# A new order of issue for the first block of an attention and gated MLP kernel

## The chip, the cores and the metric

The kernel runs on one core of one Trainium2 chip. The core has five engines, each with its own queue of instructions that it works off in order: TensorE (PE, matrix products; PEld is its weight load), VectorE (DVE), ScalarE (ACT), GpSimd (POOL) and SyncE (SP), which here issues the loads and most stores. SBUF is the working memory with 128 partitions; PSUM holds the results of TensorE in eight banks of 512 float32 columns. The metric is device time in microseconds (us). Before the change, three runs took 926.85, 927.66 and 929.27 us; the median is 927.66.

## The reference

Attention over eight batches of eight heads, 576 positions of 64 numbers, and then a gated MLP over all 4608 rows of 512 numbers:

```python
scores = q @ k.T / 8                      # per batch and head
heads 0-3: keep 0 <= rel < 32             # local: the last 32 positions
heads 4-7: keep rel >= 0, same pos % 32   # strided
attn = softmax(scores) @ v                # (8, 8, 576, 64)
x    = attn laid out as (4608, 512)
out  = (sigmoid(x @ w_gate) * (x @ w_val)) @ w_out    # 512 -> 1536 -> 512
```

All inputs and outputs are float32.

## The kernel before

**Attention** is done for pairs of heads. A batch has four pairs, numbered 0 to 3: 0 and 2 are local, 1 and 3 strided. A pair's scores are small products of its queries and keys (up to 64 columns each), laid into two banks over a mask that another product has put there. DVE takes the row maximum and subtracts it, ACT takes the exponential, DVE sums the rows and takes the reciprocal, DVE or POOL multiplies; TensorE turns the result (in batch 0) or DVE does (later), ACT copies it from PSUM, and TensorE weighs the values with it in 44 or 72 tiny products. The outcome is one of the four 128-row chunks of the MLP's input for that batch.

**The MLP** takes 512 rows of a batch at a time against 12 units of 128 hidden columns. Every product of float32 numbers is made of three faster ones: both factors are split into a high and a low part, and high x high, high x low and low x high are summed. Three such matmuls of 512 columns for one 128-row chunk of the input are called a *quarter product* here; four chunks make a gate or value product of one unit. Batches 3 to 7 use a scheme with fewer products, which the change leaves alone.

**Weights** are loaded raw (512 KB per matrix and unit, three matrices per unit) and split during the first and second batch: ACT makes an upper and a lower word (line 257 and line 261), DVE shifts (265), DVE or POOL puts them together (269), ACT rounds the high part (273), and DVE or POOL subtracts to get the low part (276).

**The order of the work** is one list, `ORDER` (line 78), of some 2360 short names. The program goes through it once and calls one function per name (`STEPS`); every instruction of the step is appended to the queue of its engine. So the list fixes the order on each engine, and semaphores make an engine wait where its next instruction needs something that another has not finished. Loads of all kinds share SP's queue. The names for the first block, `b.p` being batch and pair, `f.i` unit and matrix (0 gate, 1 value, 2 output):

- `K` constants; `fQ`, `fQa`, `fQb` load of queries and keys (whole, first part, second part); `fV` load of values; `wr` load of raw weights (all on SP)
- `C` identity matrix on POOL; `fZ` clears paddings on POOL
- `fK`, `fKa` mask and `fS`, `fSa` scores (PE); `fA`, `fAa` maximum, `fU`, `fUa` subtraction (DVE); `fE`, `fEa` exponential (ACT); `fN` sum and reciprocal (DVE); `fW` multiplication on DVE, `fWp` on POOL; `fT` transposes (PE); `fP` their copy (ACT); `fX` weighing (PE); `fH` high part (ACT) and `fL` low part (DVE) of the MLP's input; `fR` rows kept for the end (ACT); `fB`, `fM` transposes and masks on DVE in batch 1
- `wa`, `wb` upper and lower words (ACT); `ws` shift (DVE); `wd` on DVE or `wdp` on POOL, put together; `wu` high part (ACT); `wl` on DVE or `wlp` on POOL, low part
- `fg f.i.c` quarter product of batch 0, where c is the pair whose chunk it takes; `fg f.i` all four
- `s` sigmoid, `m` gating, `x`, `y` split of the hidden rows, `o` output product; `e` eviction of an output, `d` its store
- `J n` fill: matmuls of n columns of ones whose result nobody reads. They go to a tile in bank g, the same bank that `fg 0.0` uses, and need only a tile of ones that POOL sets at `J0`.

`BANKS` (line 64) says which pair of PSUM banks (a, o0 or o1) a step of the first block uses; a step not named there uses a. A step that writes a bank waits until the readers of its former contents are done. The step's instructions: a fill of 512 columns is a float32 matmul at line 730; scores are line 371, masks 358, transposes 467 and 471, weighing 513, gate and value products 592, output products 623.

Of the kernel before, what the change touches and what calls it, by code (L numbers as in the profile page):

```python
# [90 lines left out]
wd6.1 wr8.1 x0.4 y0.4 wu6.1 ws5.2 wa7.0 wlp6.1 o0.3 wd5.2 s0.5 wb7.0 wb7.1 ws7.0 wu5.2 wa7.1 wl5.2 fg5.1 ws7.1 wb6.2 wd7.1 wd7.0 wu7.1 fA1.1 wu7.0
wlp7.1 fg6.0 wa6.2 m0.5 ws6.2 x0.5 wa8.1 y0.5 wb8.1 wd6.2 fg6.1 wr9.0 wl7.0 s0.6 wu6.2 ws8.1 wb8.0 wl6.2 fU1.1 wa7.2 wa8.0 fg7.0 m0.6 wr8.2 ws8.0 x0.6
ws7.2 wb7.2 y0.6 wd8.0 fg7.1 wd7.2 s0.7 wu8.0 wd8.1 wu7.2 wl8.0 wl7.2 o0.4 m0.7 fE1.1 wa8.2 fN1.1 wb8.2 wu8.1 ws8.2 wr9.1 fWp1.1 wa9.0 fg8.0 wb9.0
ws9.0 x0.7 wr9.2 wdp8.2 fB1.1.2 fB1.1.3 o0.5 wlp8.1 s0.8 wu8.2 fB1.1.1 wlp8.2 wb9.1 wa9.1 fB1.1.0 wr10.0 fg8.1 wa9.2 wb9.2 ws9.1 wd9.1 wr10.1 wd9.0
wu9.1 y0.7 wu9.0 wlp9.1 o0.6 wl9.0 m0.8 wa10.0 fS1.2 ws10.0 wb10.1 ws9.2 wdp9.2 wb10.0 fg9.0 fM1.2 fQ1.3 wa10.1 wr10.2 x0.8 wdp10.0 wr11.0 fA1.2 wu9.2
fU1.2 wlp9.2 wu10.0 o0.7 y0.8 fE1.2 wlp10.0 fn1.2 fg9.1 fN1.2 s0.9 fW1.2 wa10.2 wb10.2 ws10.1 wd10.1 wr11.1 wa11.0 fX1.1 ws10.2 wb11.0 ws11.0 m0.9
wu10.1 wdp11.0 wr11.2 o0.8 fH1.1 fV1.2 fR1.1 fL1.1 x0.9 wlp10.1 fB1.2.0 wdp10.2 wu11.0 fB1.2.3 fg10.0 wlp11.0 fB1.2.1 wu10.2 fB1.2.2 wb11.1 fS1.3
s0.10 y0.9 fZ1.3 wlp10.2 wa11.1 fg10.1 fM1.3 LQ0 fA1.3 fU1.3 fX1.2 ws11.1 fE1.3 m0.10 wdp11.1 fN1.3 fg11.0 fH1.2 fV1.3 fR1.2 fW1.3 wu11.1 x0.10
wlp11.1 fB1.3.3 o0.9 fB1.3.2 s0.11 wb11.2 fL1.2 wa11.2 fB1.3.0 fg11.1 fB1.3.1 y0.10 ws11.2 fX1.3 m0.11 wd11.2 x0.11 o0.10 fH1.3 LV0 y0.11 wu11.2 fL1.3
pa0.0.0 fR1.3 wl11.2 pa0.0.1 g1.0 pl0 pb0.0.0 v1.0 s1.0 pb0.0.1 oh0.11.0 m1.0 x1.0 S0.0 e0.0 y1.0 d0.0 oh0.11.1 LQ1 M0.0 M0.1 D0 A0 g1.1 U0 e0.1 E0  # L100
d0.1 e0.2 N0 v1.1 d0.2 W0 s1.1 B0.3 g1.2 m1.1 e0.3 x1.1 B0.1 ph0.0.0.1 d0.3 y1.1 v1.2 B0.0 s1.2 B0.2 ph0.0.1.0 Z1 o1.0 m1.2 pw0.0.0 x1.2 pw0.0.1
pd0.0.0 y1.2 pd0.0.1 X0.0 S1.0 LV1 H0 R0 L0 o1.1 LQ2 M1.0 pa0.1.0 M1.1 D1 A1 pa0.1.1 U1 g1.3 E1 pb0.1.0 N1 W1 v1.3 s1.3 pb0.1.1 ph0.1.0.1 B1.2 B1.0
# [965 lines left out]
```

## Time and profile before

| | |
|---|---|
| median of three runs | 927.66 us (926.85 to 929.27) |
| the profiled execution | 929.75 us, its span from first to last instruction 927.6 us |
| TensorE busy | 919.8 us, 99% of the span |
| VectorE, ScalarE, GpSimd busy | 599.9, 426.8, 179.9 us |
| fills (line 730) | 20 records, the last starting at 17.9 us |
| first quarter product | 22.82 us |
| first output product `o0.0` | 49.93 us on the chain that ended last |

A row of the profile names the line, engine, operation, what is written and from what, the count, and times. A row of the timeline starts with its start and its length in us, and ends, where the engine was idle before, with that idle time and who released it. A row of stretches gives the length, then busy time and number of instructions of PE, PEld, DVE, ACT and POOL, then the granted TensorE clock as a share of full speed (PEclk), the share of the DMA engines in use, and GB/s. TensorE counts as busy while a matmul is in it, at either clock. A float32 matmul shows as two records.

### The profile page before, as it was taken

The page shows a single profiled execution, that of the slowest core. Times are in us where ns is not written, and L with a number is a line of the kernel's source. Part 1 is how long each engine was busy: PE and PEld are TensorE (multiplying, and loading weights), DVE is VectorE, ACT ScalarE, POOL GpSimd, SP SyncE. Part 2 cuts the span into 40 slices and gives each one's busy share as a digit, 9 for nine tenths or more (in the row PEclk, how much of TensorE's full clock was granted, in tenths as well). Part 3 has the DMA queues.
Part 4 walks back from the last instruction along what each step waited for, and adds up shares of the span by engine and source line. Part 5 has one row for each costly group of instructions (what it writes and reads, how often), then busy time and mean ns, then how long its engine had stood idle before and what let it go on. Part 6 is the DMA issues. An engine that isn't in the chain of part 4 may idle for free.

```text
span 927.6 us, 18516 instructions
## 1 busy us (share of the span) xinstructions
PE 919.8 (99%) x7606; PEld 754.9 (81%) x7606; DVE 599.9 (65%) x959; ACT 426.8 (46%) x776; POOL 179.9 (19%) x243
## 2 busy tenths in 40 slices
...
PEclk9899999999999999999999999999999999999999
...
GB/s 345 333 220 85 197 152 153 159 192 159 199 240 247 115 187 191 208 189 181 193 157 181 149 109 195 198 181 148 138 156 125 23 174 178 145 150 146 59 45 46
DMA packets 90195, 154.19 MB, mean 166 GB/s; under 512 B 5888, under 2 KB 40192, under 8 KB 90112
## 3 DMA queue, kind: packets, MB, share of 16 engines
...
## 4 chain that ended last, share of the span: by engine, by line
PE 98%; ACT 1%; DVE 1%; issue 0%; POOL 0%; DVEq 0%; ACTq 0%; POOLq 0%
PE o L623 22%; PE p L887 21%; PE d L887 16%; PE g L592 10%; PE v L592 10%; PE o_a L623 5%; PE o_g L623 3%; PE o_v L623 3%; PE x_a L513 2%; PE x L513 1%; PE s_g L371 1%; PE s_v L371 1%; PE gv L592 1%; PE s L371 1%; PE unread L730 0%; ACT sb L435 0%
## 5 line engine op out<-in xcount | busy, mean ns | idle before, releaser
L887 PE MATMUL p<-xs,ring 128*128 128x512 f32 x864 | 204.6, 389 | 0.0
L887 PEld LDWEIGHTS p<-xs,ring 128*128 128x128 f32 x864 | 162.2, 188 | 33.7
L623 PE MATMUL o<-w,hh 128*128 128x512 f32 x576 | 180.6, 395 | 0.0
L887 PE MATMUL d<-xs,ring 128*128 128x512 f32 x648 | 155.6, 389 | 0.0
L887 PEld LDWEIGHTS d<-xs,ring 128*128 128x128 f32 x648 | 121.6, 188 | 25.2
L623 PEld LDWEIGHTS o<-w,hh 128*128 128x128 f32 x576 | 106.1, 188 | 22.7
L480 DVE STREAM_TRANSPOSE pt<-sb 32x320 f32<-32x320 f32 (+1 forms) x224 | 120.1, 536 | 4.5
L623 PE MATMUL o<-w,hl 128*128 128x512 f32 x288 | 112.0, 389 | 0.0
L921 DVE TENSOR_TENSOR e<-e,d 128x512 f32<-128x512 f32 x54 | 37.1, 687 | 110.6 <-PE d L887 62.5
L592 PE MATMUL g<-xh,w 128*128 128x512 f32 x256 | 85.9, 393 | 0.0
L916 ACT COPY e<-p 128x512 f32<-128x512 f32 x54 | 31.7, 587 | 116.8 <-PE p L887 116.8
L592 PE MATMUL v<-xh,w 128*128 128x512 f32 x256 | 85.2, 390 | 0.0
L623 PEld LDWEIGHTS o<-w,hl 128*128 128x128 f32 x288 | 54.1, 188 | 11.5
L592 PEld LDWEIGHTS g<-xh,w 128*128 128x128 f32 x256 | 48.5, 189 | 10.3
L592 PEld LDWEIGHTS v<-xh,w 128*128 128x128 f32 x256 | 48.0, 188 | 10.0
L815 POOL TENSOR_TENSOR sum<-sum 128x128 f32<-128x128 f32 x96 | 51.5, 540 | 6.3
L592 PE MATMUL g<-xl,w 128*128 128x512 f32 x128 | 50.3, 393 | 0.3 <-DVE xl L553 0.3
L616 DVE TENSOR_TENSOR hl<-hid,hh 128x512 fp32r<-128x512 f32 x36 | 28.0, 780 | 34.5 <-ACT hh L612 34.3
L592 PE MATMUL v<-xl,w 128*128 128x512 f32 x128 | 49.8, 389 | 0.0
L810 POOL TENSOR_TENSOR sum<-w 128x256 f32<-128x256 f32 x44 | 35.5, 827 | 72.7 <-DMA sets<-sum 49.4
L929 ACT ACTIVATE e<-e 128x512 f32<-128x512 f32 x54 | 34.2, 633 | 29.9 <-DVE e L921 29.9
L612 ACT CAST hh<-hid 128x512 fp32r<-128x512 f32 x36 | 22.4, 622 | 49.9 <-PE o_a L623 41.1
...
## 6 DMA issues: line engine op xcount, KB each, us to landing
ring<-sets SPq DMA_DIRECT2D x126, 512.0 KB, 4.1
raw<-in_w_all SPq DMA_DIRECT2D x36, 512.0 KB, 5.8
vv<-in_v_l SPq DMA_DIRECT2D x15, 640.0 KB, 4.6
qk<-in_qk_l SPq DMA_DIRECT2D x14, 608.0 KB, 5.2
...
```

Source lines behind the costliest of these rows:

```text
L371: nc.tensor.matmul(sc[j % len(sc)][g * m : (g + 1) * m, j // len(sc) * BANK + (s - lo) * kk : j // len(sc) * BANK + (s - lo + 1) * kk], q[ ...
L480: nc.vector.transpose(dst[to : to + LB, :, col : col + LB], src[part * LB : (part + 1) * LB, :, h * LB : (h + 1) * LB])
L513: nc.tensor.matmul(at_bank(r, (u * per + g) * m, (u * per + g + 1) * m)[j * D : (j + 1) * D], v[part][rows, slot * P + j * D : slot * P + ...
L592: nc.tensor.matmul(o, w, x, start=first and n == 0, stop=last and n == len(todo) - 1)
L616: by.tensor_tensor(hl, whole_h.pop((k, f)), hh.bitcast(F32), op=ALU.subtract)
L623: nc.tensor.matmul(acc[k][i], h[:, i * P : (i + 1) * P], w, start=f == 0 and n == 0, stop=f == NF - 1 and n == 2,)
L810: nc.gpsimd.tensor_tensor(u[:, at : at + 2], part(wh[f][i], c), part(wl[f][i], c), op=ALU.add)
L815: nc.gpsimd.tensor_tensor(u[:, to], u[:, x], u[:, y], op=op)
L887: nc.tensor.matmul(to, w[:, (wi * 2 + c) * P : (wi * 2 + c + 1) * P], x[xi][:, c], start=p in (1, 2, 5) and c == j == 0, stop=c == 1 and j ...
L916: nc.scalar.copy(x, two[m, 0])
L921: nc.vector.tensor_tensor(x, x, two[m, 1], op=ALU.add)
L929: nc.scalar.activation(x, x, AF.Sigmoid)
```

## The change

The list is replaced from its first step up to the last steps of the weights and sums of unit pairs (batch 2's last MLP units); from there on it is the same but for single steps. No function changes, and no step's work; the names differ in these ways:

- Fills: J576, J352, J1024, J1088, J256 and J256 are replaced by J384, J160, J1184, J160, J128, J480 and J160.
- Loads: the constants come first, pair 0.2 is loaded ahead of 0.1, and weights 0.1, 0.0, 1.0 and 1.1 come ahead of 2.0 and 2.1; before it was 2.0, 1.0, 0.0, then the values, then 0.1 and 1.1.
- Order of the pairs on the engines: 0.0, 0.2, 0.1, 0.3, with the transposes and the weighing of 0.0 ahead of the scores of 0.1 and 0.3.
- The multiplication of pair 0.2 goes to POOL, those of 0.0, 0.1 and 0.3 to DVE (before: 0.0 and 0.1 on POOL); that of pair 1.3 goes to POOL.
- Weights: `wd` 20 to 17, `wdp` 16 to 19, `wl` 15 to 19, `wlp` 21 to 17 instructions.
- `BANKS`: the banks that the first block's steps use are given anew.
- Further on, six evictions `e` and their stores `d` stand one or a few places earlier (e2.2, e3.2, e4.2, e5.2, e6.3, e7.3 with their neighbours), and two rounding steps of sums (`ph`) use another buffer.

```diff
-    "S0.0": "o0", "T0.0": "o1", "X0.0": "o1", "S0.1": "o1", "T0.1": "o0", "X0.1": "o0", "S0.2": "o1", "X0.2": "o1", "T0.3": "o0", "X0.3": "o0",
+    "Sa0.0": "o0", "S0.0": "o1", "T0.0": "o0", "S0.1": "o1", "T0.1": "o1", "T0.2": "o0", "X0.2": "o0", "S0.3": "o0", "T0.3": "o0", "X0.3": "o0",
...
-fQb0.0 fZ0.0 fZ0.1 J0 K fZ0.3 fZ0.2 fQa0.0 fQa0.1 fQb0.1 wr2.0 fQ0.2 wr1.0 fQ0.3 C J576 fK0.1 wr0.0 fV0.1 fKa0.0 fV0.0 fK0.0 fV0.2 J352 fSa0.0 fV0.3 wr0.1 fS0.0
-fAa0.0 wr1.1 fSa0.1 fA0.0 fQ1.0 wr0.2 fUa0.0 wr2.1 fS0.1 fU0.0 fEa0.0 wr1.2 fK0.3 fE0.0 fA0.1 wb2.0 wa2.0 fU0.1 wr4.1 fN0.0 fE0.1 J1024 fK0.2 fS0.2 fN0.1
-fWp0.0 wa1.0 wb1.0 fA0.2 fWp0.1 wr3.1 fU0.2 J1088 fS0.3 ws1.0 fE0.2 ws2.0 wdp1.0 fT0.1 fN0.2 wa0.0 wb0.0 ws0.0 J256 fT0.0 fA0.3 wr2.2 fP0.1 wdp0.0 wu1.0 fW0.2
-J256 fX0.1 fP0.0 wlp1.0 wu0.0 fU0.3 fX0.0 fH0.1 wd2.0 fR0.1 wlp0.0 fE0.3 fL0.1 fT0.2 fH0.0 fV1.0 fR0.0 wu2.0 fL0.0 fN0.3 wlp2.0 fg0.0.0 fP0.2 fX0.2 fW0.3
-wb0.1 wa0.1 fg1.0.0 fH0.2 ws0.1 wr3.0 wb1.1 fT0.3 fL0.2 wa1.1 wd0.1 fR0.2 wr3.2 ws1.1 fg0.0.1 fP0.3 wd1.1 fS1.0 wu0.1 wu1.1 wl0.1 wb0.2 wlp1.1 fg1.0.1
-fM1.0 fQ1.1 wa0.2 fg0.1.0 fA1.0 wr4.0 fg0.0.2 wa2.1 fU1.0 fg0.1.1 wb2.1 ws2.1 fX0.3 fE1.0 wr4.2 ws0.2 wdp2.1 wb1.2 fn1.0 fg1.1.0 fH0.3 fN1.0 wu2.1
-fg0.1.2 fL0.3 fWp1.0 wa1.2 fg1.1.1 fR0.3 ws1.2 wr5.0 fg1.0.2 wlp2.1 fB1.0.1 fg0.0.3 fg0.1.3 fB1.0.0 s0.0 wdp0.2 fg1.0.3 wb2.2 m0.0 wa2.2 fg1.1.2
-wdp1.2 fB1.0.2 x0.0 wr5.1 fg2.0.0 s0.1 fg2.1.0 y0.0 wu0.2 fg2.0.1 wu1.2 fB1.0.3 wa3.0 fg1.1.3 wb3.0 ws2.2 fZ1.1 fg2.1.1 m0.1 wdp2.2 wr5.2 fg2.0.2
-wl0.2 x0.1 fX1.0 wb3.2 y0.1 wa3.1 ws3.0 fg2.1.2 fH1.0 fV1.1 wd3.0 wb3.1 fg2.0.3 ws3.1 fR1.0 fL1.0 wr6.0 fg2.1.3 wdp3.1 s0.2 fS1.1 wu3.0 m0.2 wlp3.0
-wu3.1 wl1.2 x0.2 o0.0 fQ1.2 wa4.0 wa3.2 wl3.1 wb4.0 wr6.1 y0.2 wu2.2 wr6.2 ws4.0 wb4.1 fg3.0 wlp2.2 wd4.0 wa4.1 wr7.0 wa4.2 ws3.2 wu4.0 ws4.1 wdp3.2
...
+J0 K fZ0.0 fZ0.1 fQa0.0 fZ0.3 fZ0.2 fQb0.0 fQ0.2 wr0.1 wr0.0 C J384 fK0.2 fQb0.1 fKa0.0 fV0.0 fK0.0 wr1.0 fSa0.0 fQa0.1 wr1.1 fQ0.3 fS0.0 fAa0.0 fA0.0 fV0.2
+fUa0.0 J160 fS0.2 fV0.1 fU0.0 fEa0.0 fV0.3 wr2.0 fE0.0 fA0.2 wr2.1 fQ1.0 wa0.1 fN0.0 wr0.2 wb0.1 wr1.2 wr3.0 fW0.0 wb0.0 wa0.0 fU0.2 J1184 fT0.0 wr2.2 ws0.1
+fK0.1 ws0.0 fP0.0 fE0.2 wd0.0 J160 fX0.0 wu0.0 fN0.2 wb1.0 fV1.0 wd0.1 fH0.0 fWp0.2 J128 fSa0.1 fR0.0 wa1.0 fL0.0 wl0.0 wr3.1 wa1.1 J480 fT0.2 wb1.1 ws1.1 fS0.1
+wr3.2 ws1.0 wdp1.1 fP0.2 fA0.1 wu0.1 J160 fK0.3 fU0.1 fS0.3 wlp0.1 wu1.1 fg0.0.0 fE0.1 fA0.3 wdp1.0 fg0.1.0 fU0.3 fN0.1 wlp1.1 wu1.0 fE0.3 fW0.1 wa2.0
+wlp1.0 wb2.0 fN0.3 fT0.1 wa2.1 wr4.1 fX0.2 fP0.1 fW0.3 wb2.1 ws2.0 fX0.1 fH0.2 ws2.1 wr4.2 wdp2.0 fR0.2 fL0.2 fH0.1 fT0.3 fR0.1 fL0.1 wdp2.1 wu2.0
+fS1.0 fP0.3 wl2.0 fg0.0.1 wu2.1 fQ1.1 fM1.0 wa0.2 wlp2.1 fg0.1.1 wb0.2 fA1.0 fg1.1.0 wb3.0 wr4.0 fg1.0.0 fU1.0 wa3.0 fg0.1.2 ws0.2 wr5.2 fE1.0 ws3.0
+wdp0.2 fg1.1.1 wb1.2 fn1.0 fX0.3 wa1.2 fN1.0 fg0.0.2 wr5.0 fH0.3 ws1.2 fWp1.0 fg1.1.2 wu0.2 fL0.3 fR0.3 fg1.0.1 wa3.2 wb3.2 fg0.0.3 wlp0.2 fB1.0.0
+fg0.1.3 wr6.1 fB1.0.1 wdp3.0 fg1.1.3 s0.0 fg1.0.2 wa3.1 m0.0 wdp1.2 fg2.0.0 fB1.0.3 x0.0 fg2.1.0 wu3.0 fg2.0.1 y0.0 wa4.0 wlp3.0 fB1.0.2 fg2.1.1 wb3.1
+wb4.0 fg1.0.3 wr6.0 ws3.1 fZ1.1 wr6.2 fg2.0.2 s0.1 ws4.0 fX1.0 wu1.2 wdp4.0 m0.1 wd3.1 x0.1 fg2.1.2 fV1.1 fH1.0 y0.1 fR1.0 fS1.1 wu3.1 fL1.0 wu4.0
+wlp3.1 fg2.0.3 fQ1.2 wb2.2 wl1.2 fg2.1.3 s0.2 wlp4.0 o0.0 wa2.2 m0.2 wa4.1 wr5.1 x0.2 ws4.1 wb4.1 y0.2 wa5.0 wr7.0 wd4.1 fg3.0 wb5.0 ws5.0 wu4.1 wr7.2
+ws3.2 wlp4.1 wd3.2 wdp5.0 o0.1 s0.3 ws2.2 wu3.2 wb5.1 wa5.1 wl3.2 wr8.0 wd2.2 wu5.0 fg4.0 wu2.2 wl5.0 ws5.1 wa6.0 wdp5.1 wb6.0 ws6.0 fg3.1 wu5.1 wl2.2
...
-d6.0 e6.1 d6.1 e6.2 G7.0.1 d6.2 V7.0.1 e6.3 c7.0.0.1 d6.3 G7.0.2 r75 c7.0.1.1 V7.0.2 ad7.0.0.2 sg7.0.2 G7.0.6 r76 ad7.0.1.2 mu7.0.2 V7.0.6 c7.0.0.6
+d6.0 e6.1 d6.1 e6.2 d6.2 G7.0.1 e6.3 d6.3 V7.0.1 c7.0.0.1 G7.0.2 r75 c7.0.1.1 V7.0.2 ad7.0.0.2 sg7.0.2 G7.0.6 r76 ad7.0.1.2 mu7.0.2 V7.0.6 c7.0.0.6
```

More of the change, by code (lines that the diff above doesn't have):

```diff
@@ L91 @@
[L91 to L102, printed above, removed]
@@ new lines @@
+wlp3.1 fg2.0.3 fQ1.2 wb2.2 wl1.2 fg2.1.3 s0.2 wlp4.0 o0.0 wa2.2 m0.2 wa4.1 wr5.1 x0.2 ws4.1 wb4.1 y0.2 wa5.0 wr7.0 wd4.1 fg3.0 wb5.0 ws5.0 wu4.1 wr7.2
+ws3.2 wlp4.1 wd3.2 wdp5.0 o0.1 s0.3 ws2.2 wu3.2 wb5.1 wa5.1 wl3.2 wr8.0 wd2.2 wu5.0 fg4.0 wu2.2 wl5.0 ws5.1 wa6.0 wdp5.1 wb6.0 ws6.0 fg3.1 wu5.1 wl2.2
+wlp5.1 fM1.1 wb4.2 wa4.2 fA1.1 wdp6.0 wr7.1 wb6.1 o0.2 m0.3 wa6.1 fU1.1 x0.3 s0.4 y0.3 wu6.0 ws4.2 wlp6.0 ws6.1 fS1.2 fg4.1 fE1.1 fQ1.3 wdp4.2 wb7.0
+fN1.1 wa7.0 wu4.2 ws7.0 fWp1.1 fg5.0 m0.4 x0.4 wdp7.0 fB1.1.2 y0.4 wdp6.1 wu7.0 fg5.1 fB1.1.3 fB1.1.0 wlp4.2 s0.5 wu6.1 o0.3 wlp6.1 wa5.2 m0.5 fB1.1.1
@@ new lines @@
+x0.5 wlp7.0 wa7.1 wb7.1 fM1.2 wb5.2 fg6.0 ws7.1 fA1.2 wa8.0 wdp7.1 wr8.1 wb8.0 fU1.2 wr8.2 wu7.1 y0.5 fX1.1 s0.6 wl7.1 o0.4 ws5.2 fV1.2 wd5.2 fE1.2
+ws8.0 wdp8.0 wu5.2 fn1.2 wa8.1 fg6.1 wl5.2 wb8.1 fN1.2 wr9.0 wa6.2 fW1.2 wb6.2 wu8.0 ws6.2 ws8.1 fR1.1 wdp6.2 o0.5 fH1.1 m0.6 fB1.2.0 x0.6 wu6.2 y0.6
+wl6.2 fg7.0 wd8.1 wb7.2 wl8.0 wa7.2 wu8.1 ws7.2 wb9.0 wd7.2 fg7.1 wl8.1 fB1.2.1 s0.7 wu7.2 fL1.1 wa9.0 o0.6 m0.7 wr9.2 wl7.2 x0.7 wb8.2 y0.7 wa8.2
+ws9.0 wd9.0 fg8.1 wr9.1 fB1.2.2 wu9.0 wl9.0 ws8.2 wd8.2 fg8.0 wb9.1 fB1.2.3 wa9.1 wu8.2 fZ1.3 ws9.1 wr10.0 wd9.1 o0.7 wl8.2 s0.8 wu9.1 m0.8 wa9.2
@@ new lines @@
+wlp9.1 wb9.2 ws9.2 wa10.0 wr10.1 fg9.0 wb10.0 ws10.0 x0.8 wd10.0 wr10.2 y0.8 wu10.0 wd9.2 wlp10.0 fS1.3 s0.9 wb10.1 fg9.1 fM1.3 LQ0 wa10.1 wu9.2
+ws10.1 wr11.0 wd10.1 wl9.2 wu10.1 fg10.0 m0.9 wb10.2 wl10.1 x0.9 y0.9 wa11.0 fA1.3 wb11.0 fg10.1 s0.10 wr11.2 ws11.0 wa10.2 wd11.0 fU1.3 wr11.1 wu11.0
+wl11.0 o0.8 m0.10 fE1.3 ws10.2 x0.10 wdp10.2 fN1.3 wb11.1 y0.10 wa11.1 fWp1.3 fX1.2 wu10.2 ws11.1 o0.9 fH1.2 fV1.3 wlp10.2 fR1.2 fB1.3.2 fB1.3.1
+wdp11.1 fg11.0 fL1.2 wu11.1 fB1.3.0 fB1.3.3 o0.10 s0.11 wl11.1 wa11.2 wb11.2 ws11.2 wd11.2 fX1.3 fg11.1 fH1.3 LV0 wu11.2 fL1.3 fR1.3 wl11.2 pa0.0.1
@@ new lines @@
+g1.0 m0.11 x0.11 pb0.0.1 y0.11 v1.0 s1.0 pa0.0.0 pb0.0.0 pl0 oh0.11.0 m1.0 x1.0 S0.0 e0.0 y1.0 d0.0 oh0.11.1 LQ1 M0.0 M0.1 D0 A0 g1.1 U0 e0.1 E0 d0.1
+e0.2 N0 v1.1 d0.2 W0 s1.1 B0.2 g1.2 B0.1 e0.3 m1.1 ph0.0.0.1 d0.3 B0.3 x1.1 v1.2 y1.1 B0.0 s1.2 ph0.0.1.0 Z1 o1.0 m1.2 pw0.0.0 x1.2 pw0.0.1 pd0.0.0
+y1.2 pd0.0.1 X0.0 S1.0 LV1 H0 pa0.1.0 R0 o1.1 LQ2 M1.0 M1.1 pa0.1.1 D1 A1 U1 pb0.1.0 g1.3 L0 E1 N1 pb0.1.1 ph0.1.0.1 W1 v1.3 B1.1 s1.3 ph0.1.1.0 B1.3
+o1.2 m1.3 B1.0 x1.3 y1.3 B1.2 g1.4 pw0.1.0 pw0.1.1 pd0.1.0 pd0.1.1 v1.4 s1.4 pa1.0.0 g1.5 m1.4 pa1.0.1 x1.4 pl1 y1.4 pb1.0.0 v1.5 s1.5 pb1.0.1
```

57 lines of the change are left out of this document (27 added, 30 removed).

## The prediction

> **What bounds the kernel now.** I read the page first: engines, the clock by slices, and the chain that ended last.
>
> ```profile
> span 927.6 us, 18516 instructions
> PE 919.8 (99%) x7606; PEld 754.9 (81%) x7606; DVE 599.9 (65%) x959; ACT 426.8 (46%) x776; POOL 179.9 (19%) x243
> PEclk9899999999999999999999999999999999999999
> PE 98%; ACT 1%; DVE 1%; issue 0%; POOL 0%; DVEq 0%; ACTq 0%; POOLq 0%
> ```
>
> TensorE is the bound nearly everywhere; the only low clock is in the second slice. Next come TensorE's waits over the whole span (waiter, releaser, us in total, times, longest).
>
> ```profile
> PE t L467 <- POOL sb L459: 0.6, 1, 0.6
> PE x L513 <- issue: 0.5, 1, 0.5
> ...
> ```
>
> These are the longest after the start; three more of 0.2 to 0.3 us follow, and the last of all ends before 24 us. Then busy time and granted clock by stretch (PEclk is the third value from the end).
>
> ```profile
> 20.00:30.00 10.00, 9.20 (x161) 7.37 (x158) 7.47 (x15) 6.47 (x19) 4.23 (x3) 0.69 1.02 408
> 30.00:40.00 10.00, 10.00 (x159) 7.88 (x158) 8.14 (x18) 9.20 (x21) 5.77 (x5) 0.97 1.00 385
> 40.00:50.00 10.00, 10.00 (x155) 8.03 (x154) 9.69 (x17) 8.59 (x18) 5.18 (x7) 1.00 0.64 191
> 60.00:70.00 10.00, 10.00 (x46) 8.29 (x45) 9.44 (x14) 8.35 (x16) 6.62 (x5) 1.00 0.40 131
> ...
> 16.90:20.32 3.42, 2.94 (x81) 2.15 (x79) 3.38 (x6) 3.42 (x9) 2.92 (x3) 1.00 1.04 404
> 20.32:23.74 3.42, 2.62 (x62) 1.90 (x57) 3.08 (x7) 2.92 (x12) 2.92 (x3) 1.00 1.02 411
> 23.74:27.16 3.42, 3.42 (x75) 2.71 (x75) 1.98 (x4) 1.40 (x4) 0.99 (x1) 0.50 1.02 404
> ...
> 23.70:23.80 0.10, 0.10 (x1) 0.10 (x2) 0.10 (x1) 0.10 (x2) 0.10 (x1) 0.74 1.06 417
> 30.50:30.60 0.10, 0.10 (x1) 0.10 (x1) 0.00 (x0) 0.10 (x2) 0.00 (x0) 0.62 0.77 307
> ```
>
> The clock fell to 0.50 at about 23.75 us and came back at about 30.57: 6.8 us at half speed, 3.4 us lost. After that TensorE is gapless to the end. The change can therefore win or lose only in the first 32 us, unless its new order makes a later product wait. Since TensorE's work is the same in both lists except for the fill matmuls, the question is when it reaches one given state. The chain gives that state:
>
> ```profile
> 7.11 0.62 DVE mx L409 x2
> ...
> 9.00 1.28 ACT L435
> ...
> 24.77 2.41 PE x L513 x72
> ...
> 28.76 1.28 PE t L467 x6
> ...
> 31.04 0.97 PE s L371 x64
> ...
> 32.90 0.69 PE v L592 x3
> ...
> 45.53 1.29 PE x L513 x72
> ...
> 49.93 2.94 PE o L623 x12
> ```
>
> At 32.0 us the old list has done the four pairs' scores, their transposes, three of their four weighings, the scores of 1.0, and three quarter products. Where the new list starts fg0.0.1 it has done all of that but one quarter product (0.69 us). My **mark** is the start of fg0.0.1: 32.0 − 0.69 = 31.3 us is what the new list has to beat. Every us at the mark is a us at the first `o` (49.93) and at the end.
>
> **The early part.** Constants and queries of 0.0 go ahead of the keys of 0.0. These rows are issues on SP (start, length) and landings (KB, us from issue) of single loads:
>
> ```profile
> 1.65 0.43 SPq L303 DMA_DIRECT2D qk<-in_qk_l  x1
> 6.85 0.41 SPq L236 DMA_DIRECT2D raw<-in_w_all  x1
> 9.10 0.33 SPq L316 DMA_DIRECT2D vv<-in_v_l  x1
> 15.91 0.33 SPq L303 DMA_DIRECT2D qk<-in_qk_l  x1
> ...
> qk<-in_qk_l SPq DMA_DIRECT2D x1, 400.0 KB, 4.2
> raw<-in_w_all SPq DMA_DIRECT2D x1, 512.0 KB, 9.0
> vv<-in_v_l SPq DMA_DIRECT2D x1, 640.0 KB, 9.3
> qk<-in_qk_l SPq DMA_DIRECT2D x1, 608.0 KB, 9.8
> ```
>
> The queries of 0.0 are issued one slot (0.45 us) earlier and have 208 KB less ahead of them; the old first score also stood behind a fill. So the first max on DVE moves from 7.11 to about 6.2. Then the table load, exponential, sum, weights and transpose follow as before: T0.0 at 12.4, X0.0 at 13.9 to 15.2.
>
> That gain ends at the loads. DMA is full from 16.9 to 40 us (shares near 1.0, the last value but one), so a landing follows the bytes issued before it. The 640 KB row landed at 18.4 us, with 5089 KB issued up to and including it; the 608 KB row at 25.7 with 7745 KB. That is 364 KB/us. (The twentieth load went out at 15.9, when the twelfth, the 512 KB row, landed at 15.85: eight are under way, so SP holds the later ones back, but the bytes decide.) Counting the new list's loads by this line: raw weights 1.0 at 14.8, queries 0.1 at 15.7, weights 1.1 at 17.1, queries 0.3 at 18.8, weights 2.0 at 24.0, weights 2.1 at 25.4.
>
> Where do these stand in a queue? ACT has wb1.0 ahead of fH0.0, wa1.1 ahead of fP0.2, and wa2.1 ahead of fP0.1. Prices:
>
> ```profile
> 8.84 0.82 DVE L409 TENSOR_REDUCE mx<-s 128x12 f32<-128x648 f32 x1
> 9.69 0.83 DVE L418 TENSOR_TENSOR sb<-s,mx 128x648 f32<-128x648 f32 x1
> 23.49 0.83 DVE L441 TENSOR_REDUCE mxs<-sb 128x12 f32<-128x660 f32 x1
> 24.35 0.23 DVE L451 RECIPROCAL mxs<-mxs 128x12 f32<-128x12 f32 x1
> 24.62 0.83 DVE L459 TENSOR_TENSOR sb<-sb,mxs 128x648 f32<-128x648 f32 x1
> 17.12 0.65 ACT L261 ACTIVATE low<-raw 128x512 int32<-128x512 uint32 x1
> 17.68 0.82 ACT L489 COPY pt<-t 128x512 f32<-128x512 f32 x2
> 22.15 0.59 ACT L549 CAST xh<-x 128x512 fp32r<-128x512 f32 x1 [0.50 <-PE x L513]
> 32.05 1.31 POOL L276 TENSOR_TENSOR w<-words,w 128x512 fp32r<-128x512 f32 x1 [7.32 <-ACT w L273]
> ```
>
> ACT: wa1.1 17.1 to 17.7, wb1.1 to 18.3, fP0.2 to 19.0. The bank of fK0.3 is free only then, so fS0.3 ends at 20.3. fg0.0.0 and fg0.1.0 follow at 0.69 each, to 21.7. DVE takes fA0.3 from 20.35, fU0.3, fN0.1, fW0.1 (0.85, 0.83, 1.07, 0.85): done at 23.95. T0.1 needs fW0.1, so **TensorE idles 21.7 to 23.95, 2.25 us**. No fill can stand there, as the fills write bank g, which fg0.0.0 holds. X0.2 then runs 24.7 to 26.0. wa2.1 waits for its load until 25.4, so fP0.1 ends at 26.9 and X0.1 waits 0.9 us. T0.3 shares its bank with X0.2 and waits for fL0.2 (28.75, behind wb2.1 and fH0.2). With T0.3 and fS1.0, the mark is 30.45 at full clock, −0.85 us. If weights 2.1 land in time the mark is 29.2 (−2.1). These are the two bounds at full clock. As a floor, DVE's own steps up to fL0.1 (4 maxima, 4 subtractions, 4 sums, 3 multiplies, and 12 weight or split steps of 0.4 to 0.7) are some 20 us of work from 6.2, with 1.4 idle at the table load: 27.6, or −3.7.
>
> **The clock.** Between 20.3 and 23.75 TensorE was busy 77% in the old run with no gap above 0.5 us, and still lost its clock. The next stretch, full but of tiny weighing matmuls for the most part, did not bring it back; the one after did, with products again. The new list has 2.25 us idle, then only transposes and 54 to 72 tiny matmuls until the mark. I take the clock as lost, at about 26 us. Cold, 72 weighings cost 2.41 instead of 1.29, a factor 1.87: X0.1 26.95 to 28.55, T0.3 28.8 to 30.05, fS1.0 to 31.85. The return takes a denser stretch, say 34.5 us, so products run 2.65 us at half speed: 1.3 lost. Mark-equivalent 33.2, or +1.9; with weights 2.1 in time +1.1. I take **+1.5**. Bounds of this term: nothing (clock kept) and return at 37.8 (+3.5).
>
> A rule speaks for a kept clock: the Trainium skill, "TensorE: Matmul & The Clock Gate", section "HAM oscillation — how this bites in real kernels", warns only of idle gaps above about 3.4 us. By it the 2.25 us gap would cost no clock. This trace disagrees, with its drop after gaps of at most 0.6 us.
>
> **Parts costed at nothing.** The start fills (J384 for J576) and the seven others sit in waits. Moving multiplies and weight steps between DVE and POOL (wd 20 to 17, wdp 16 to 19, wl 15 to 19, wlp 21 to 17) and reordering units 2 to 11 are covered by TensorE's 0.69 us products, which wait for nothing from 24 us on. The cover is thin: DVE 94 to 97% busy in the rows above; one late POOL step would cost up to 1.31 us. Eviction ahead of its copy and store (e2.2, e3.2, e4.2, e5.2, e6.3, e7.3) swaps a 0.6 us ACT or DVE step; the store order on SP stays. Nothing, either way.
>
> **Rivals.**
> *A: the clock holds,* because the two quarter products and the transposes suffice. For it: 16.9 to 20.3 us kept full speed with transposes and weighings. Against: those had a fill among them. −0.85 to −2.1, middle −1.4: 926.3.
> *B: slower.* The clock returns one stretch later. It decides if half speed lasts past 36.3 us: then at least 2.2 us are lost on products, from +2.8; at 37.8, +3.5. Middle 3.2: 930.9. For it: the stretch after the drop in the old run was full of matmuls, yet did not bring the clock back.
> *C: the loads land later than counted,* so the fills end before the waits do: 1 us more on weights 1.1 moves everything from 17.1 on, and gives +2.5, 930.2. Against it: the two landings of the line are 7 us apart and bracket most of these.
>
> **How the numbers follow.** The profiled run took 929.75 us, 2.15 outside its span and 2.09 above the median 927.66. I add differences to the median: 927.66 + 1.5 = 929.2. If that 2.09 is itself a cold clock that the other runs didn't have, the new time is later by up to that. Forecast 0.45, A 0.27, B 0.18, C 0.10. About 0.3%, 2.8 us, can be told from no change: faster is below 924.9, slower above 930.4. Faster needs A beyond its bounds, near DVE's floor: 0.11. Slower: B, a third of C, and the forecast's upper end: 0.26. Same: 0.63. The range runs from A's better bound to past B: 925.4 to 931.4; the forecast's own is 928.0 to 930.5.
>
> **What would show it.** Right: first DVE max near 6.2 us; a TensorE wait of about 2 us before T0.1 on DVE or POOL; one before X0.1 on ACT; clock 0.50 from about 26 us for two or three stretches; then no wait. Wrong: full clock throughout (A); T0.1 less than 1 us after fg0.1.0; or a wait of a product on POOL or DVE after 35 us, which I hold to be absent.

## The result, and the profile after

The kernel before took 927.93 us (median of four runs, 926.85 to 929.27), the changed one 939.88 us (four runs, 938.15 to 940.29): a ratio of 1.0126, 95% interval 1.0114 to 1.0139. It is slower by about 11.9 us; 929.2 was forecast, with 931.4 as the upper end of the range. The profiled execution took 938.15 us, its span 936.1.

The stretches of the changed kernel at the start (length, busy time of the five engines, granted clock, DMA share, GB/s) and, with its idle time, the rows of TensorE that the prediction had named:

```profile
22.00:24.00 2.00, 0.32 (x3) 0.32 (x4) 1.93 (x4) 1.68 (x4) 2.00 (x2) 1.00 1.02 411
24.00:26.00 2.00, 2.00 (x79) 1.83 (x77) 1.93 (x5) 1.93 (x6) 0.78 (x2) 0.90 1.01 406
26.00:28.00 2.00, 1.51 (x52) 1.33 (x46) 0.87 (x2) 1.66 (x6) 2.00 (x2) 0.50 1.05 414
...
34.00:36.00 2.00, 2.00 (x6) 1.52 (x6) 1.87 (x4) 1.76 (x4) 1.07 (x1) 0.54 0.99 389
36.00:38.00 2.00, 2.00 (x11) 1.36 (x10) 0.76 (x4) 0.35 (x1) 1.53 (x2) 1.00 1.03 409
```

```profile
23.68 0.33 PE L467 MATMUL t<-ident,sb 128*128 128x128 f32 x1 [2.18 <-DVE sb L459]
...
28.02 1.33 PE L467 MATMUL t<-ident,sb 128*128 128x128 f32 x5 [0.52 <-DVE xl L553]
30.06 0.48 PE L467 MATMUL t<-ident,sb 128*128 128x128 f32 x1 [0.71 <-issue]
...
31.80 0.79 PE L592 MATMUL g<-xh,w 128*128 128x512 f32 x1
...
52.83 0.39 PE L623 MATMUL o<-w,hh 128*128 128x512 f32 x1
```

T0.1 waits 2.18 us, half speed lasts from about 25.6 to 35.8 us, and `fg0.0.1` starts at 31.80: the start went nearly as forecast. What was not forecast lies 200 us later. The same view for 240 to 280 us, first before, then after the change:

```profile
240.00:250.00 10.00, 10.00 (x84) 8.13 (x84) 9.65 (x17) 4.05 (x7) 6.65 (x13) 1.00 0.45 153
...
270.00:280.00 10.00, 10.00 (x157) 8.32 (x155) 9.60 (x17) 3.95 (x6) 7.51 (x14) 1.00 0.44 145
```

```profile
240.00:250.00 10.00, 9.72 (x129) 7.94 (x122) 7.33 (x15) 4.97 (x13) 5.85 (x10) 1.00 0.99 304
250.00:260.00 10.00, 8.70 (x148) 7.11 (x147) 9.55 (x17) 5.89 (x11) 3.88 (x8) 1.00 0.51 160
260.00:270.00 10.00, 9.06 (x40) 7.18 (x39) 8.66 (x15) 4.71 (x7) 6.89 (x12) 1.00 0.66 197
270.00:280.00 10.00, 8.34 (x152) 6.62 (x151) 8.52 (x14) 5.32 (x13) 5.80 (x8) 1.00 0.90 269
```

TensorE had no gap there; now it idles 0.28 + 1.30 + 0.94 + 1.66 = 4.2 us, at a granted clock of 1.00 throughout. Its waits over the whole span (us in total, times, longest):

```profile
PE o L623 <- DVE ob L639: 1.4, 1, 1.4
...
PE x_a L513 <- DVE pt L480: 1.3, 2, 0.7
...
PE g L592 <- ACT e L600: 0.9, 1, 0.9
```

These are an output product that waits for the eviction of its bank, weighings that wait for transposed probabilities, and a gate product that waits for ACT. Behind them stand two waits on other engines, here in the timelines of DVE and ACT:

```profile
238.80 1.25 DVE L824 TENSOR_TENSOR sum<-sum,sumh 128x512 fp32r<-128x512 f32 x1 [4.13 <-ACT sumh L820]
```

```profile
262.12 0.59 ACT L639 COPY ob<-o 128x512 f32<-128x512 f32 x1 [1.50 <-DMA sets<-sumh]
...
268.13 0.59 ACT L639 COPY ob<-o 128x512 f32<-128x512 f32 x1 [3.52 <-DMA out<-ob]
```

The names are those of the sums of weights that batches 3 to 7 need: `pa`, `pb` add on GpSimd, `ph` rounds on ACT (line 820), `pw` subtracts on DVE (824), `pd` stores. The evictions `e1.x` of batch 1 (639) and the rounded sums share two buffers (`ost` and `l0`). In the new list the sums of pair 3 stand earlier and the evictions later: `pw3.1.0` is ahead of the maxima of the fourth scores on DVE, and an eviction finds its buffer still held by a store.

### The profile page after: what moved, and what is told of

Same layout as the page of the kernel before. It is cut to its first block, busy times and chain, and to the rows that moved or that the text cites. A ratio compares the mean times of both kernels' runs of the same rounds, so it can differ in the third digit from the quotient of the medians.

```text
span 936.1 us, 18504 instructions
## 1 busy us (share of the span) xinstructions
PE 920.1 (98%) x7604; PEld 754.5 (81%) x7604; DVE 597.6 (64%) x960; ACT 428.2 (46%) x776; POOL 176.1 (19%) x242
## 4 chain that ended last, share of the span: by engine, by line
PE 88%; DMA 4%; ACT 2%; POOL 2%; DVE 2%; issue 1%; SPq 1%; ACTq 0%; POOLq 0%; DVEq 0%
PE p L887 21%; PE o L623 20%; PE d L887 16%; PE g L592 8%; PE v L592 8%; PE o_a L623 5%; PE o_g L623 3%; PE o_v L623 3%; PE x_a L513 2%; POOL sum L815 1%; DMA sets<-sum 1%; DMA qk<-in_qk_s 1%; DMA raw<-in_w_all 1%; PE s_g L371 1%; PE s_v L371 1%
## 5 line engine op out<-in xcount | busy, mean ns | idle before, releaser
L623 PE MATMUL o<-w,hh 128*128 128x512 f32 x576 | 180.6, 395 | 1.4 <-DVE ob L639 1.4
L623 PEld LDWEIGHTS o<-w,hh 128*128 128x128 f32 x576 | 106.2, 188 | 24.2 <-DVE ob L639 1.6
L623 PE MATMUL o<-w,hl 128*128 128x512 f32 x288 | 112.0, 389 | 0.0
L623 PEld LDWEIGHTS o<-w,hl 128*128 128x128 f32 x288 | 54.1, 188 | 11.5
L616 DVE TENSOR_TENSOR hl<-hid,hh 128x512 fp32r<-128x512 f32 x36 | 28.0, 780 | 34.5 <-ACT hh L612 34.3
L329 POOL MEMSET sb<- 128x12 f32 (+1 forms) x18 | 2.1, 119 | 230.0 <-DVE pt L480 230.0
```

Source lines behind the costliest of these rows:

```text
L616: by.tensor_tensor(hl, whole_h.pop((k, f)), hh.bitcast(F32), op=ALU.subtract)
L623: nc.tensor.matmul(acc[k][i], h[:, i * P : (i + 1) * P], w, start=f == 0 and n == 0, stop=f == NF - 1 and n == 2,)
```

## The experiments

In the kernels below the list takes six text lines less, so their line numbers are six lower (L617 is L623). Only the unchanged kernel of e7 keeps the old ones. Ratios are to the kernel before on the same chip, with 95% intervals.

### The two halves of the list

The lists can be cut at `oh0.11.0`, where the same steps have been issued in both (but for the engine of some multiplications and weight steps, and the fills).

```diff
 e1: ORDER = new list up to oh0.11.0 (with the new banks) + old list from there on
 e2: ORDER = old list up to oh0.11.0 (with the old banks) + new list from there on
```

> New list up to the first output steps of batch 1's eleventh unit (oh0.11.0), old list from there on; the banks are the new ones. Theory (the loss has two places, the start with its lost clock and the sums of weights in batches 1 and 2): the first output product comes 3 us later than before as in the changed kernel (52.8 against 49.9), nothing waits after that, so 3 us slower than before, 931. Rival (the sums of weights wait because the start hands over a bad state): as slow as the changed kernel, 940. Rival (the start costs nothing at the end, since later slack takes it up): no change.

> Old list up to oh0.11.0, new list from there on, old banks. Theory (two places): TensorE waits between 240 and 280 us on evictions and exponentials as in the changed kernel, some 5 to 8 us; 933 to 936. Rival (bad state handed over by the start): no waits after 31 us and no change against before.

Measured: e1 933.2 us, 1.0064 (1.0049 to 1.0079); e2 934.06 us, 1.0069 (1.0054 to 1.0084), against 927.6. The halves lose 5.6 and 6.5 us, together 12.1, and the whole change loses 11.9. So there are two places. e1 lost more than the 3 us that were expected of it; the next experiment shows why. All four executions of e1, like all four of the changed kernel, have a mean granted clock of 0.994 or 0.995, so the new start loses its clock each time. e2 has no wait of the changed start, and still loses; its stretches:

```profile
245.00:250.00 5.00, 3.42 (x24) 2.41 (x22) 4.82 (x9) 2.12 (x3) 3.28 (x6) 1.00 0.37 128
250.00:255.00 5.00, 4.89 (x112) 4.50 (x113) 4.15 (x8) 3.40 (x7) 0.24 (x2) 0.52 0.37 105
```

TensorE idles 1.6 us, and in this execution the clock then falls to half as well. It did not in all of them: the one of four with a mean clock of 1.000 took 931.66 us. In the changed kernel the same place cost 4.2 us of idle time at full clock. So the second loss is made up differently in the two kernels, and that the halves add up so closely is partly luck.

### Was the profile of before typical?

e7 is the kernel before, unchanged, profiled again. e4 is the kernel before with two more fills in its waits, e6 that with the start of the new list:

```diff
 e4:
-... fX0.0 ... fT0.2
+... J160 fX0.0 ... J384 fT0.2
 e6, beside e4's fills:
-fQb0.0 fZ0.0 fZ0.1 J0 K fZ0.3 fZ0.2 fQa0.0 ... J576 ... J352
+J0 K fQa0.0 fZ0.0 fZ0.1 fZ0.3 fZ0.2 fQb0.0 ... J384 ... J64
```

> The kernel before, unchanged, profiled a second time. Theory (the cold stretch of 6.8 us in the first profile belonged to that execution and not to the kernel): granted clock 1.0 in all slices or a loss of at most one stretch of 3.4 us, first o at 47.2 to 48.5, 926.8 to 928.5. Rival (the list before does lose its clock at 23.75 us in most executions): clock 0.50 from about 24 to 30 us and first o at 49.9 again, 929 to 930.

> The kernel before, with fills of 160 columns ahead of X0.0 and 384 columns ahead of T0.2, in bank g, 0.9 us of TensorE work of which about 0.6 us stand in waits. If a few more matmuls in the stretch from 20.3 to 23.7 us keep the clock: no stretch at half speed, 2 to 3 us faster than before, 925. If the clock is lost anyway: 0 to 0.5 us slower.

> The list before, with only the start of the new one: constants and the queries of pair 0.0 ahead of its keys, fills J384 and J64 for J576 and J352, and the two fills J160 ahead of fX0.0 and J384 ahead of fT0.2. Theory (the first maximum is reached sooner and in the old list nothing on DVE or ACT stands between it and the first products): first maximum at 5.5 to 6.2 instead of 7.1, first o at 46.5, 926.6 to 927.0. Rival (loads of the weights bound the start of the first products, so the earlier maximum is hidden): 927.6 to 928.0.

Measured: e7 927.37 us (span 925.2); e4 927.78, 1.0001 (0.9991 to 1.0011); e6 927.5, 1.0002 (0.9993 to 1.0011). The stretches of e7, then its last scores (`fS1.0`) and its first output product:

```profile
22.00:24.00 2.00, 1.47 (x17) 0.80 (x20) 1.93 (x6) 2.00 (x6) 1.99 (x2) 1.00 1.04 412
24.00:26.00 2.00, 2.00 (x73) 1.79 (x70) 1.31 (x3) 1.10 (x3) 0.00 (x0) 1.00 1.00 397
26.00:28.00 2.00, 2.00 (x80) 1.59 (x79) 1.97 (x4) 2.00 (x6) 0.00 (x0) 1.00 1.05 420
```

```profile
27.31 0.30 PE L371 MATMUL s<-qk 64*32 64x64 f32 x10
...
46.54 0.50 PE L623 MATMUL o<-w,hh 128*128 128x512 f32 x1
```

The clock stays at 1.00 up to 920 us, and the first output product comes at 46.54 us; in the timeline of the first profile it stands at 49.86. Put as the prediction put it, the mark is the end of fS1.0, 27.31 + 1.04 at full clock, less one quarter product: **27.66 us, not 31.3**. The cold stretch of 6.8 us belonged to that execution.

One profile could be the exception itself, but the mean clock of many more executions is known. Of 77 executions of the kernel before that were timed beside the experiments, 64 have a mean clock of 0.999 or more, with a median of 927.4 us. Nine have 0.996 or less, with a median of 929.9; the first profile, with 0.996 and 929.75 us, is one of that kind.

Fills therefore bring the median nothing: all ten executions of e4 have a clock of 0.999 or more, and its time is unchanged, so the hoped-for 925 was missed. e6's profile has its first output product at 46.53 us, as its theory said, but that is no sooner than e7's 46.54, and the time is the rival's: the theory of a gain there fell.

### What the new start costs

e3 is e1 with a fill in the wait before T0.1. The prediction said that no fill could stand there because bank g is held; e3 writes it to bank a. e8 is e3 with pair 0.1's sum and multiplication ahead of pair 0.3's subtraction. e11 is e3 with the words of weights 2.0 and 2.1 moved behind pairs 0.2 and 0.1.

```diff
 e3:
-... wa2.0 wlp1.0 wb2.0 fN0.3 fT0.1
+... wa2.0 wlp1.0 wb2.0 fN0.3 Ja1250 fT0.1
 e8, against e3:
-fU0.3 fN0.1 wlp1.1 wu1.0 fE0.3 fW0.1 wa2.0 wlp1.0 wb2.0 fN0.3 Ja1250 fT0.1
+fN0.1 fW0.1 fU0.3 wlp1.1 wu1.0 fE0.3 wa2.0 wlp1.0 wb2.0 fN0.3 Ja700 fT0.1
 e11, against e3:
-wa2.0 wlp1.0 wb2.0 fN0.3 Ja1250 fT0.1 wa2.1 wr4.1 fX0.2 fP0.1 fW0.3 wb2.1 ws2.0 fX0.1 fH0.2 ws2.1 wr4.2 wdp2.0 fR0.2 ...
+wlp1.0 fN0.3 Ja1250 fT0.1 wr4.1 fX0.2 fP0.1 fW0.3 fX0.1 fH0.2 wr4.2 fR0.2 fL0.2 fH0.1 fT0.3 fR0.1 wa2.0 wb2.0 ws2.0 wdp2.0 wa2.1 wb2.1 ...
```

> The first kernel of this call, with a fill of 1250 columns ahead of T0.1, written to bank a, which nothing holds at that point; it fills the 2.2 us wait there. Theory A (the clock is lost because of that wait): the clock stays at full speed or is lost one stretch later, and 1.7 to 3.4 us come back against the same list without the fill. Theory B (the clock is lost because of the weighings and transposes, which count for little): the clock still falls at about 25 to 28 us for three stretches, and the fill changes less than 1 us.

> The third kernel (new list up to oh0.11.0, old list after it, with a fill in bank a; 930.62 us), with the sum and multiplication of pair 0.1 (fN0.1, fW0.1) ahead of the subtraction of pair 0.3 (fU0.3), and the fill before fT0.1 cut to 700 columns. Theory (the subtraction and maximum of pair 0.3 ahead of them on DVE make T0.1 late, and that sets the mark): T0.1 0.8 us sooner, the start of fg0.0.1 0.8 to 0.9 us sooner, 929.7. Rival (ACT's queue, with the words of weights 2.1 waiting for their load ahead of fH0.2, sets T0.3 and the mark): T0.1 sooner but T0.3 waits longer, 930.4 to 931.

> The third kernel (new list up to oh0.11.0 with a fill of 1250 columns in bank a, old list after it; 930.62 us), with the words, shifts and joins of weights 2.0 and 2.1 moved behind the steps of pairs 0.2 and 0.1 (wa2.0, wb2.0, wa2.1, wb2.1 behind fR0.1 on ACT). Theory (ACT's queue sets fP0.1, fH0.2 and with them T0.3 and the mark): T0.3 and the start of fg0.0.1 about 1.0 us sooner, no wait for the split at T0.3 over 0.5 us, 929.6. Rival (DVE's chain of maxima, subtractions and sums sets them): T0.3 no sooner, 930.4 to 930.9.

Measured: e3 930.62 us, 1.0034 (1.0023 to 1.0045); e8 933.99, 1.0068 (1.0052 to 1.0084); e11 931.53, 1.0042 (1.0027 to 1.0056). In e3's profile the clock holds at 1.00 although TensorE still waits. Two stretches, then the mark and the first output product:

```profile
26.00:28.00 2.00, 1.45 (x76) 1.21 (x70) 0.71 (x3) 2.00 (x7) 1.48 (x2) 1.00 1.01 404
28.00:30.00 2.00, 1.24 (x49) 1.07 (x52) 1.82 (x5) 1.68 (x8) 1.07 (x1) 1.00 1.06 422
```

```profile
30.53 0.50 PE L586 MATMUL g<-xh,w 128*128 128x512 f32 x1
...
49.73 0.39 PE L617 MATMUL o<-w,hh 128*128 128x512 f32 x1
```

The mark is 30.53 us, where the prediction had 30.45 for a full clock. That is 2.9 later than 27.66, and the time is 3.0 longer. So the start's 5.6 us are 2.6 of clock, which the fill gives back, and 3.0 of later order, which it does not. (Five of e3's seven executions have a clock of 0.999 or more, with a median of 929.9 us; two have 0.996 and 0.997.)

e8 got worse, by more than either theory allowed. The rows of its DVE and GpSimd, and two of TensorE's waits:

```profile
22.72 1.69 DVE L453 TENSOR_TENSOR sb<-sb,mx 128x648 f32<-128x648 f32 x1
```

```profile
22.44 1.27 POOL L270 TENSOR_TENSOR w<-words,w 128x512 fp32r<-128x512 f32 x1
23.67 1.86 POOL L270 TENSOR_TENSOR w<-high,w 128x512 fp32r<-128x512 f32 x1
```

```profile
PE x L507 <- ACT pt L483: 1.4, 1, 1.4
...
PE t L461 <- DVE sb L453: 1.0, 1, 1.0
```

The multiplication took 1.69 us where it had taken 1.03 in e3 (the next multiplication took 0.83 in both), so T0.1, at 24.46 us against 24.22 in e3, was no sooner. And the subtraction of pair 0.3, now behind it, let ACT's exponential fE0.3 start at 25.18 instead of 22.79 us, with everything queued behind that: the words of weights 2 and fP0.1. The edit moved a wait from DVE to ACT, and the clock was lost too (0.995 or 0.996 in all four executions). Whether the shorter fill or the new waits of 1.0 to 1.4 us lost it, this run does not separate.

e11 did what its theory said at the mark, and gave it back:

```profile
29.33 0.50 PE L586 MATMUL g<-xh,w 128*128 128x512 f32 x1
```

```profile
PE g L586 <- ACT xh L543: 0.7, 1, 0.7
PE g L586 <- ACT e L594: 0.6, 1, 0.6
...
PE g L586 <- DVE xl L547: 0.4, 1, 0.4
```

The mark is 1.2 us sooner, but quarter products now wait 0.7, 0.4 and 0.6 us at 37.5, 38.4 and 41.8 us, probably because the words stand ahead of later steps on ACT. So the first output product comes at 50.62 us, 0.9 later than in e3. The time is that of e3 within the intervals.

### What the new rest costs

e5 moves four steps of the sums in e2. e9 takes e2 and puts the sums of pairs 3 to 5 and the evictions `e1`, `d1` at their old places; e10 is e9 with the sums of pair 3 new again; e12 is the head of e11 with the rest of e9.

```diff
 e5, against e2 (the stretch around the fourth scores):
-X3.0 y1.11 S4.0 ph3.1.0.0 pa3.1.1 LV4 H3 pw3.1.0 R3 oh1.9.1 LQ5 M4.0 pd3.1.0 L3 ... E4 g2.0 ph3.1.1.0 N4
+X3.0 y1.11 S4.0 pa3.1.1 LV4 H3 R3 oh1.9.1 LQ5 M4.0 L3 ... E4 ph3.1.0.0 pw3.1.0 pd3.1.0 g2.0 N4 W4 v2.0 s2.0 ph3.1.1.0
 e9, against e2 (the evictions; the sums of pairs 3 to 5 likewise):
-... E4 ... B4.3 m2.0 ... D5 U5 pa4.0.1 e1.1 E5 xl3.0.1 d1.1 e1.0 ... d1.0 ... B5.0 e1.2 ... R5 e1.3
+... E4 ... B4.3 e1.0 d1.0 m2.0 ... D5 e1.2 U5 d1.2 ... e1.1 ... oh2.0.0 e1.3
```

> The old list up to oh0.11.0 and the new list after it, as in the second of the spliced lists (934.06 us), but the four steps ph3.1.0.0, pw3.1.0, pd3.1.0 (rounded sums of batch 3) moved behind E4, and ph3.1.1.0 behind s2.0, so that DVE's subtraction for a sum no longer stands ahead of the maximum of pair 1.4's scores. Theory (DVE waits for a sum of ACT ahead of M4.0, so X4.0 is late, and after that TensorE loses a clock stretch): no wait of 0.5 us or more at X4.0, granted clock 1.0 from 240 to 260, 4 to 5 of the 6.5 us back, 929 to 930. Rival (the evictions and their stores, which use the same two buffers as the sums, hold ACT's queue): 933 to 934 as before, ACT's waits for stores of 1.3 to 3.5 us still there and x_a waits of 1.3 us with them.

> The old list up to oh0.11.0 and the new list after it, but with the steps of the rounded sums of pairs 3, 4 and 5 (names pa, pb, ph, pw, pd, pl) and the evictions and stores of batch 1 (e1, d1) at their places of the old list; the sums 0 to 2, the transposes and the later evictions stay as in the new list. Theory (these sums and evictions hold the whole loss of the second place): 927.3 to 928.3, TensorE without waits over 0.3 us between 200 and 300. Rival (the loss is spread over all the moves): 929.5 to 931.

> The kernel of the run e9_rest_old_sums, with the steps of the sums of pair 3 alone at their places of the new list (the subtraction pw3.1.0 ahead of the maxima of the fourth scores, and the rounded sums earlier on ACT). Theory (two causes that add: DVE held by a sum that ACT has not rounded, about 2.4 us as moving it brought, and the evictions behind stores, about 4): 929.8 to 930.6, the wait of TensorE for a transposed tile before X4.0 back. Rival one (evictions and stores alone): under 928.3. Rival two (the sums of pair 3 alone, which also push the evictions): 933 to 934.

> The head of e11_head_act_order and the rest of e9_rest_old_sums: the new list with the fill in bank a, the words of weights 2 moved, and the sums 3 to 5 and evictions of batch 1 at their old places. Theory (the places add): e11's time plus what e9 stands above the kernel before, 929.6 to 930.0. Rival (a place only shows in company of the other, through the phase of the clock): 931 or more, or 928 or less.

Measured: e5 931.61 us, 1.0043 (1.0028 to 1.0058): 2.4 of the 6.5 us back, less than the theory said, and the rival is not right either. The waits of the weighings fell from 1.7 to 0.4, but others stayed or came:

```profile
PE o L617 <- DVE ob L633: 1.1, 1, 1.1
PE g L586 <- ACT e L594: 1.0, 1, 1.0
...
PE s_v L365 <- DVE e L599: 0.5, 1, 0.5
```

e9 938.11 us (1.0116, 1.0098 to 1.0134), e10 941.27 (1.0144, 1.0128 to 1.0161) and e12 941.78 (1.0150, 1.0135 to 1.0166) were slower than e2, against every expectation. The reason lies in the splice itself; here in e9:

```profile
321.09 0.79 PE L586 MATMUL g<-xh,w 128*128 128x512 f32 x1 [8.10 <-ACT e L594]
```

The splits of batch 3's input (`xd3`, `xh3`, `xl3`) stood at their new, earlier places, and the sums of pair 5 at their old, later ones. `xd3` and these sums share a buffer: GpSimd's `xd3` at 312.91 us waited 9.89 us for the store of a sum, and ACT 6.64 us for `xd3`. In the window that was to be tested e9 is clean, full from 200 to 270 us and with 0.09 us of idle time after that:

```profile
270.00:280.00 10.00, 9.91 (x154) 8.14 (x153) 9.60 (x18) 6.33 (x11) 3.95 (x9) 1.00 0.23 63
```

So the three say nothing by their times. They were done again with the splits at their old places as well, e16 with the head of e3:

```diff
 e13 = e9  with xd3, xh3, xl3 at their old places
 e14 = e13 with the sums of pair 3 at their new places
 e16 = head of e3 (with Ja1250) + rest of e13
 e15, against e13, the evictions alone late:
-... B4.3 e1.0 pb3.1.1 d1.0 ... D5 e1.2 U5 d1.2 ... e1.1 N5 W5 d1.1 ... oh2.0.0 e1.3 pw4.0.0 d1.3
+... U5 e1.1 xl3.0.1 E5 d1.1 e1.0 v2.1 pa4.0.0 N5 d1.0 W5 ... B5.0 e1.2 g2.2 m2.1 d1.2 ... R5 e1.3 LQ7 M6.0 d1.3
```

> The kernel of e9_rest_old_sums, with the splits of batch 3's input (xd3, xh3, xl3) at their places of the old list too, so that GpSimd does not do xd behind the sums of pair 5. Theory (the loss of the second place lies in the sums 3 to 5 and the evictions e1; the other moves cost nothing): no wait of 8 us at 313, 927.3 to 928.3. Rival (the other moves, sums 0 to 2 and the later evictions, cost too): 929.5 or more, with waits of TensorE outside the start.

> The kernel of e13_rest_old_sums_x, with the sums of pair 3 at their places of the new list. Theory (two causes that add): 2.4 to 3.2 us above e13, 930.0 to 931.2, with the wait for a transposed tile before X4.0 of about 1.4 us and a cold stretch after it. Rival one (evictions alone): equal to e13. Rival two (the sums of pair 3 alone): 6 us above e13.

> The head of the third kernel (new list up to oh0.11.0 with a fill of 1250 columns in bank a; 930.62 us with the old rest) and the rest of e13_rest_old_sums_x. Theory (the two places add, and what is left is the later mark of the new head, 30.5 instead of 27.3 to 28.2 us): 930.3 to 931.3. Rival (the new rest makes up for a later start in its slack): 928.5 or less.

> The kernel of e13_rest_old_sums_x (927.67 us), with the evictions and stores of batch 1 (e1, d1) alone at about their places of the new list: e1.1 behind U5, e1.0 behind E5, e1.2 behind B5.0, e1.3 behind R5. Theory (the evictions are late for the output products of batch 2, which need their banks, and hold ACT behind stores, whatever the sums do): 931 to 932.5, a wait of an output product for an eviction of 1 us or more. Rival (they cost only in company of the earlier sums 4, whose rounded parts lie in the same two buffers and have to be stored first): 927.4 to 928.5, no such wait, and no wait of ACT for a store of over 1 us.

| | median, us | ratio (95%) |
|---|---|---|
| e13 | 927.67 | 0.9999 (0.9989 to 1.0010) |
| e14 | 929.07 | 1.0015 (1.0003 to 1.0026) |
| e16 | 929.91 | 1.0022 (1.0010 to 1.0034) |
| e15 | 933.62 | 1.0061 (1.0047 to 1.0075) |

**e13 gives the whole of the second place back.** The sums of pairs 0 to 2, the transposes and the six later evictions, which stay new in it, cost nothing that shows beyond the interval. e14 shows the wait that its theory named, and its profile the cold stretch (a clock of 0.66 from 250 to 255 us), at a lower price, 1.4 us:

```profile
PE x_a L507 <- DVE pt L474: 1.4, 2, 0.8
```

e15 loses 6.0 us by late evictions alone. TensorE's waits, those of ACT and of DVE between 200 and 330 us, and the stretches:

```profile
PE x_a L507 <- DVE pt L474: 2.1, 3, 0.8
...
PE o L617 <- DVE ob L633: 1.0, 1, 1.0
```

```profile
ACT sumh L814 <- DMA out<-ob: 4.2, 1, 4.2
```

```profile
DVE sum L818 <- ACT sumh L814: 9.7, 4, 4.5
```

```profile
275.00:280.00 5.00, 2.56 (x23) 1.68 (x25) 4.79 (x10) 0.34 (x1) 3.32 (x8) 0.86 0.19 56
280.00:285.00 5.00, 5.00 (x113) 4.51 (x114) 4.20 (x7) 3.92 (x8) 0.20 (x3) 0.50 0.59 142
```

Read together, these rows give a chain: a late eviction's store holds the buffer, ACT waits 4.2 us to round the next sum into it, DVE's subtraction of that sum stands ahead of the softmax, the weighings are late, and the clock drops to half. The causes don't add: the sums of pair 3 alone cost 1.4, evictions alone 6.0, all together 6.5, and e5 lost 4.3 with those sums moved. How the new list's 6.5 us divide is therefore not settled. Buffers of their own for the evictions were not tried.

e16, with the fill in the start and the old places in the rest, is 2.0 us above before, a little under the 930.3 that its theory gave and within the intervals of e3. No version beat the kernel before by more than its runs differ.

## Why the prediction was wrong

**The start, step by step: right.** First maximum 5.47 us (6.2 said), T0.0 at 11.76 (12.4), X0.0 at 13.32 (13.9), the idle time before T0.1 2.18 (2.25), clock lost at 25.6 (26), `fg0.0.1` at 31.80 (31.85). Weights 2.1 landed in time, so X0.1 didn't wait; this is the better of the two bounds, but an unforeseen 0.71 us inside T0.3, for which the profile names no releaser and which e1 does not have, took that back. That 31.80 agrees with the 31.85 of the worse bound is therefore luck. The clock returned at 35.8 instead of 34.5, between the forecast and rival B: after the mark the changed kernel needs 52.83 − 31.80 = 21.03 us to its first output product and e3 49.73 − 30.53 = 19.20, so 1.8 us were lost there (1.3 said; 52.33 − 32.41 = 19.92 in e1's profile, 0.7).

**"31.3 us is what the new list has to beat", and "I add differences to the median": wrong.** The mark held a cold stretch that the median runs mostly did not have. Against 27.66 the same working gives 33.2 − 27.66 = +5.5 where it had +1.9, and +5.1 for the +1.5 that was taken; e1 measured +5.6. The prediction named the risk in a sentence, bounded by 2.1 us, and gave it no chance. The bound was too small as well, because a microsecond at the mark is not always one at the end: the first profile is 3.7 us later than e7 at the mark, 3.3 at the first output product and 2.4 at the end of the span. The rest is lost again in e7 between 240 and 300 us. Rival A, "the clock holds", rested on the same mark: with the clock held (e3) the time is 930.6, not 926.3.

**"No fill can stand there": wrong.** Bank g was held, but bank a was free. A fill there kept the clock in e3's profile and was worth 2.6 us; e16, with the same fill, shows one cold stretch of about 3.4 us in its profile, so it doesn't always keep it.

**"Reordering units 2 to 11 ... covered by TensorE's 0.69 us products. Nothing": wrong by 6.5 us.** The products waited for nothing in the old order because the sums and evictions stood where their buffers were free. The prediction saw DVE 94 to 97% busy in rows between 40 and 70 us and called the cover thin, but never looked at ACT's and DVE's queues around 240 to 280 us; it named only the six later evictions, which cost nothing, and not those of batch 1. It did say what would prove it wrong, a wait of a product on POOL or DVE after 35 us, and that came.

**The sum.** Against e7's span of 925.2 us the changed kernel's 936.1 is 10.9 longer: 52.83 − 46.54 = 6.3 at the first output product, 4.2 of idle time from 240 to 280, 0.4 elsewhere.

**Rival C**, later loads, didn't happen: ACT's waits for raw weights 1.1 and 2.0 ended at 16.6 and 23.3 us, sooner than the 17.1 and 24.0 counted, T0.1 waited for DVE, and X0.1 not at all.
